# A_wq's first half in two requests (32 and 96 partitions), and the store's wait on GpSimd

## The chip, the cores and the metric

The kernel runs on one core of a Trainium2 chip, and the metric is the device time of one execution in microseconds (us), median of several runs. A core has TensorE (PE), VectorE (DVE), ScalarE (ACT), GpSimd (POOL) and SyncE (SP). Each has its own list of instructions and waits on semaphores. Transfers between device memory and the on-chip memory of 128 partitions are requested by an instruction on an engine, here nearly all on SyncE, and carried out by 16 DMA engines which all the queues share.

## The reference

One token is decoded. Its normalised row goes through a sliding-window attention (window 4096 of a cache of 65,536, 32 query heads, 8 K/V heads of 128) and through a gated feed-forward block of 1792, and both are added to the input.

```python
x = A_x                                   # (1, 1, 512)
xn = _layernorm(x, axis=-1)
return x + _A_ref(xn, A_k_cache, A_v_cache, A_wq, A_wo) + _B_ref(xn, B_w_r, B_w_gate, B_w_up, B_w_down)

# _A_ref: W = 4096, Hq = 32, Hkv = 8, Dh = 128
q = (x @ wq) split into heads             # wq: (512, 4096)
k, v = last W rows of each cache, each head repeated for 4 query heads
p = softmax(q k^T * Dh**-0.5);  o = p v
return o @ wo                             # wo: (4096, 512)

# _B_ref (S = 1, C = 1: the one token is always selected)
y = (silu(x @ w_gate) * (x @ w_up)) @ w_down
return x + y * sigmoid(x @ w_r)
```

## The kernel before

All weights and the window of the caches are read once, 30.67 MB in all, and there is little arithmetic on each byte. The kernel therefore requests everything early, on SyncE's queue, in the order in which it is needed: the two halves of `A_wq` (`wq0`, `wq1`, 2 MiB each), K in five pieces (`k0` and `k1` of 1 MiB for one head each, then three of 2 MiB for two heads each), V in four of 2 MiB, `w_gate` and `w_up` (1.75 MiB each), `A_wo` in two of 2 MiB, and `w_down` in four pieces of 896, 512, 256 and 128 KiB. The tensor `wq_sb` holds `A_wq` as 128 partitions x 4 blocks of 4096: a partition's row of one half (two blocks) is 16 KB in one piece. Two small rows, the token `x` and the router's weights `wr`, are requested on ScalarE.

The head. The program begins with a barrier of all engines. Two requests are taken out of the body and put ahead of it: `early` (line 103) records an instruction's name in `ahead`, and when the program is complete `hoist` (line 82) moves each such instruction into the first block, in front of its engine's drain, which is the engine's part in that barrier. These are `wq0` on SyncE and `x` on ScalarE (lines 110 and 111). `hoist` also moves the instructions that would end each engine's program, among them a further barrier, up to a place in the middle (`ends_at`; for SyncE behind the request `v0`).

The body. VectorE and ScalarE normalise `x` (lines 236 to 247), TensorE turns the row into a column (L251), VectorE and ScalarE compute the router's factor (L257 to L264), and TensorE spreads it (L266). Then TensorE computes q (L295), first with `wq0` (`kh` = 0), then, behind two filling products (L290), with `wq1`; before each half it waits for its transfer, by `PE.need(t_wq[kh], t_ps0)` (line 291). SyncE requests `w_gate` and `w_up` when q is complete.

The scores. For each of eight K/V heads VectorE copies K to a work buffer (`kin`, L334; it waits for the K transfer here), TensorE transposes it (L367), VectorE and ScalarE bring it back (`kT`, L339 and L342), and TensorE multiplies it with q (L376). A maximum over the window, an exponential (L425), the transposes of p (L431) and eight rounds with V (L442 to L489) follow.

The end. TensorE computes gate and up (L511), o through `A_wo` (L536), and the products with `w_down` (L541), each piece behind its own wait; fillers (L191, L489) are products whose results are not used. VectorE and ScalarE each bring half of the result row back (L568, L569), SyncE requests its store and waits for the landing (lines 571 and 572). `Eng.need` (line 27) puts a wait on that engine's own list; nothing follows this wait in any engine's program but its end.

```python
t_wq = [early(nc.sync, "wq0", wq_sb[:, 0:KH, :], wq_v[:, 0:KH, :])]
t_x = early(nc.scalar, "x", xrow[:], A_x.rearrange("a b d -> (a b) d"))
```

Of the kernel before, what the change touches and what calls it, by code (L numbers as in the profile page):

```python
# [38 lines left out]
def kernel(  # L39
# [14 lines left out]
    nc = tc.nc  # L54
    P = 128
# [18 lines left out]
    wq_sb = nc.alloc_sbuf_tensor("wq_sb", [P, KT, NQ], BF16)  # L74
    xrow = nc.alloc_sbuf_tensor("xrow", [1, D], BF16)
    KH = KT // 2
    wq_v = A_wq.rearrange("(p kt) n -> p kt n", kt=KT)

    ahead, ends_at = {}, {}

    @ctx.callback
    def hoist():
        tc.close()
        tc.compile()
        blocks = nc.main_func.blocks
        head = blocks[0].instructions
        for blk in blocks[1:]:
            for i in [i for i, o in enumerate(blk.instructions) if o.name in ahead][::-1]:
                ins = blk.instructions.pop(i)
                at = next(k for k, o in enumerate(head) if o.engine == ins.engine and isinstance(o, mybir.InstDrain))  # L90
                head.insert(at, ins)
        for eng, name in ends_at.items():
            tail = []
            for blk in blocks[-2:]:
                for o in [o for o in blk.instructions if o.engine == eng and not isinstance(o, mybir.InstUnconditionalBranch)]:
                    blk.instructions.remove(o)
                    tail.append(o)
            blk, at = next((b, k) for b in blocks for k, o in enumerate(b.instructions) if o.name == name)
            blk.instructions[at + 1:at + 1] = tail
# [3 lines left out]
    def early(eng, name, out_, in_):  # L103
        s = nc.alloc_semaphore("d_" + name)
        ins = eng.dma_start(out=out_, in_=in_)
        ins.then_inc(s, 16)
        ahead[ins.ins.name] = ins.ins.engine
        return (s, 16)

    t_wq = [early(nc.sync, "wq0", wq_sb[:, 0:KH, :], wq_v[:, 0:KH, :])]  # L110
    t_x = early(nc.scalar, "x", xrow[:], A_x.rearrange("a b d -> (a b) d"))
    W3, F1, F2, F3, F4 = 2, 2, 1, 1, 2

# [71 lines left out]
    PE, ACT, DVE, POOL, SP = (Eng(nc, nc.tensor, "pe"), Eng(nc, nc.scalar, "act"), Eng(nc, nc.vector, "dve"),  # L185
                              Eng(nc, nc.gpsimd, "pool"), Eng(nc, nc.sync, "sp"))
    te, ac, ve, gp, sy = nc.tensor, nc.scalar, nc.vector, nc.gpsimd, nc.sync
# [5 lines left out]
    def ends(ins):  # L193
        ends_at[ins.ins.engine] = ins.ins.name
        return ins

    def dma(eng, name, out_, in_):
        s = S("d_" + name)
        ins = eng.dma_start(out=out_, in_=in_)  # L199
        ins.then_inc(s, 16)  # L200
        if name == "v0":
            ends(ins)
        return (s, 16)

    t_wr = dma(ac, "wr", wr_row[:], B_w_r.rearrange("(a d) -> a d", a=1))
    t_wq.append(dma(sy, "wq1", wq_sb[:, KH:, :], wq_v[:, KH:, :]))
    TP = W // PH

    def pair(name, tile_, cache, i0, i1):
# [22 lines left out]
    t_ps0 = DVE.mark(ve.memset(ps[:, 0:2, :].rearrange("p a b -> p (a b)"), 0.0))  # L232
# [4 lines left out]
    a = DVE.mark(ve.bn_stats(out=stats[:], in_=xrow[:]))  # L237
# [6 lines left out]
    a = DVE.mark(ve.reciprocal(out=sml[:, 1:2], in_=sml[:, 0:1]))  # L244
# [5 lines left out]
    for kt in range(KT):  # L250
        ins = te.matmul(ps[:, 6, 256 + kt:257 + kt], lhsT=xn_row[:].rearrange("a (p k) -> a k p", k=KT)[:, kt, :],  # L251
                        rhs=ident_bf[0:1, 0:1], start=True, stop=True)
# [34 lines left out]
    for kh in range(2):  # L287
        if kh == 1:
            for ch in range(2):
                te.matmul(sc[:, ch, :], lhsT=zst[:], rhs=zmov[:], start=True, stop=False, skip_group_check=True)  # L290
        PE.need(t_wq[kh], t_ps0)
        for hf in range(2):
            for kt in range(kh * KH, (kh + 1) * KH):
                for c in range(4):
                    ins = te.matmul(ps[32 * c:32 * c + 1, hf, :], lhsT=xnT[:, kt:kt + 1],  # L295
                                    rhs=wq_sb[:, kt, (4 * hf + c) * 512:(4 * hf + c + 1) * 512],
                                    start=(kt == 0), stop=(kt == KT - 1), tile_position=(0, 32 * c))
            if kh == 1:
                t_qp = PE.mark(ins)
                ACT.need(t_qp)  # L300
                t_qe.append(ACT.mark(ac.copy(out=q4[:, hf, :], in_=ps[:, hf, :])))
    for hf in range(2):
# [3 lines left out]
        for hl in range(4):  # L306
            ins = te.transpose(qT_ps[:, hl, :], q4[:, hf, hl * DH:(hl + 1) * DH], ident_bf[:])
# [97 lines left out]
    a = POOL.mark(gp.memset(rf, 0.0))  # L405
# [8 lines left out]
    a = DVE.mark(ve.reduce_max(out=gm[:], in_=ps[0:2, 6, 0:P].rearrange("a (q c) -> a c q", q=8), axis=AX.X))  # L414
# [13 lines left out]
    for h in range(2):  # L428
        PE.need(t_p[h])
        for k in range(8):  # L430
            ins = te.transpose(tp[:, h, k * P:(k + 1) * P], p_sb[:, h, k * P:(k + 1) * P], ident_bf[:])  # L431
# [39 lines left out]
    with te.Fori(1, 9) as i:  # L471
# [4 lines left out]
        for tl in range(4):  # L476
            ins = te.matmul(pv_ps[32 * tl:32 * tl + 32, :], lhsT=pTcur[:, tl].rearrange("p q e r -> p (q e r)"),  # L477
                            rhs=vin[:, 0].rearrange("p (q t) d -> p t q d", t=4)[:, tl],
                            start=True, stop=False, tile_position=(0, 32 * tl))
        ins.then_inc(pe_pva, 1)  # L480
        te.wait_ge(s_vb, i)
        for tl in range(4):
            ins = te.matmul(pv_ps[32 * tl:32 * tl + 32, :], lhsT=pTcur[:, 4 + tl].rearrange("p q e r -> p (q e r)"),  # L483
                            rhs=vin[:, 1].rearrange("p (q t) d -> p t q d", t=4)[:, tl],
                            start=False, stop=True, tile_position=(0, 32 * tl))
        ins.then_inc(pe_pv, 1)
        collect(psf[:, bass.ds(4 * 512 + g * 8, 8)]).then_inc(pe_col, 1)
        for _ in range(W3):
# [9 lines left out]
    a = DVE.mark(ve.reduce_sum(out=oT_f[:].rearrange("p (g j) -> p g j", g=HP),  # L498
                               in_=ps[:, 4, 8:72].rearrange("p (g u j) -> p g j u", g=HP, u=2), axis=AX.X))
# [7 lines left out]
    for m in range(2):  # L507
        PE.need(t_g if m == 0 else t_u)
        for kt in range(KT):
            for c in range(4):  # L510
                ins = te.matmul(ps[32 * c:32 * c + 1, 2 + m, 0:FC], lhsT=xnT[:, kt:kt + 1],  # L511
                                rhs=wgu[:, m * KT * F + kt * F + c * FC:m * KT * F + kt * F + (c + 1) * FC],
                                start=(kt == 0), stop=(kt == KT - 1), tile_position=(0, 32 * c))
# [6 lines left out]
    a = ACT.mark(ac.activation(out=gth4[:], in_=ps[:, 2, 0:FC], func=ACTF.Tanh, scale=0.5))  # L520
# [13 lines left out]
    def grouped(j, lhsT, w):  # L534
        c = j % 4
        return te.matmul(a_ps[32 * c:32 * c + 1, :], lhsT=lhsT, rhs=w[:, j * D:(j + 1) * D], start=False, stop=False,  # L536
                         tile_position=(0, 32 * c), skip_group_check=True)

    def by_halves(lhsT, row, stop=False):
        for c in range(2):  # L540
            ins = te.matmul(g_ps[c], lhsT=lhsT, rhs=row[:, c * HD:(c + 1) * HD], start=False, stop=stop,  # L541
                            tile_position=(0, 32 * c), skip_group_check=True)
        return ins

    for k, (j0, j1) in enumerate(wo_chunks):
        PE.need(t_wo[k])
        for j in range(j0, j1):
            ins = grouped(j, oT2[:, j:j + 1], wo_sb)
# [8 lines left out]
    for k, (j0, j1) in enumerate(wd_chunks):  # L557
        PE.need(t_wd[k])
        for j in range(j0, j1):
            ins = by_halves(hTr[:, j, 0:1], wd_sb[:, j * D:(j + 1) * D], stop=(j == FB - 1))  # L560
# [8 lines left out]
    ac.copy(out=res[:, HD:], in_=g_ps[1]).then_inc(s_res, 1)  # L569
    sy.wait_ge(s_res, 2)  # L570
    t_out = dma(sy, "out", out.rearrange("a b d -> (a b) d"), res)
    SP.need(t_out)


# [28 lines left out]
```

## Time and profile before

| | |
|---|---|
| median of 3 runs | 79.16 us (78.93 to 79.17) |
| the profiled execution's own time | 79.16 us |
| its span, first to last instruction | 77.7 us |
| mean granted TensorE clock | 0.978 |
| read from device memory | 30.67 MB, 395 GB/s over the span |
| busy: PE, DVE, ACT, POOL | 72%, 57%, 39%, 13% |
| chain of waits: PE, DMA, ACT, DVE | 42%, 27%, 14%, 9% |

The profile is one execution, with times from the first instruction on. A row like the one of DMA cuts the span into 40 slices of 1.94 us, each digit a busy share in tenths. The timeline gives the start, the duration, the engine, the line and the operands of instructions, and in brackets how long the engine had been idle before and what ended that. "SPq" and "ACTq" are the request instructions themselves on SyncE and ScalarE, not the transfers. In the list of waits a row gives who waited for whom, the total, the number of times, and the longest. The windows give, for a stretch of the span, its length, each engine's busy time with its instructions, and at the end the granted clock, the busy share of the 16 DMA engines and the GB/s that they moved.

### The profile page before, as it was taken

To read this page: it belongs to the slowest core of one execution; us is meant where nothing else is said; L and a number is where in the kernel's file an instruction comes from. 1 tells how busy PE (TensorE), PEld (TensorE's weight loads), DVE (VectorE), ACT (ScalarE), POOL (GpSimd) and SP (SyncE) were. 2 spreads that over 40 slices of the span, in tenths; PEclk is the share of its full clock that TensorE was granted. 3 is DMA by queue.
4 is the path that set the end of the run, shared out by engine and by line. 5 is a ranking of instruction groups with operands and counts; after the bars stand their busy time and mean duration, and the time that the engine had idled before them with its cause. 6 is when DMAs were issued, how large, how long until landed. Compare 5 with 4: busy or idle time off the path is not lost.

```text
span 77.7 us, 1640 instructions
## 1 busy us (share of the span) xinstructions
PE 56.4 (72%) x642; PEld 29.7 (38%) x642; DVE 43.9 (57%) x96; ACT 30.4 (39%) x41; POOL 10.3 (13%) x22
## 2 busy tenths in 40 slices
PE   0010795489823999899799586778888779999991
PEld 0010401266603666577568122422322234343350
DVE  2763910488007876696696376398898914920302
ACT  2760002227940559589577505233334332000001
POOL 3950000003100302022021860000000000000000
PEclk9999999999999569999999999999999999999999
DMA  6899999999999999999999999999999999999910
GB/s 135 362 439 422 421 405 421 438 455 430 430 413 455 413 430 430 430 430 430 430 417 430 421 430 430 428 404 443 428 428 434 429 430 438 421 391 397 346 37 1
DMA packets 2745, 30.72 MB, mean 395 GB/s; under 512 B 307, under 2 KB 438, under 8 KB 822
## 3 DMA queue, kind: packets, MB, share of 16 engines
q1 hardware_dynamic: 2738, 30.67, 94.1%
q8 instruction: 2, 0.03, 0.2%
q14 instruction: 1, 0.01, 0.0%
q10 hardware_dynamic: 4, 0.00, 0.0%
HBM read 30.67 MB, written 0.00 MB: 395 GB/s over the span
## 4 chain that ended last, share of the span: by engine, by line
PE 42%; DMA 27%; ACT 14%; DVE 9%; issue 3%; SPq 2%; DVEq 0%
DMA k_sb<-in_A_k_cache_dram 27%; PE ps L367 13%; ACT kT L342 8%; PE ps L191 7%; PE ps L376 5%; ACT pvS L462 5%; PE ps L541 3%; PE ps L483 3%; PE ps L477 3%; PE ps L536 2%; DVE vin L448 2%; ACT kin L425 2%; PE ps L511 2%; SPq L199 2%; PE ps L468 2%
## 5 line engine op out<-in xcount | busy, mean ns | idle before, releaser
L342 ACT COPY kT<-ps 128x1024 bf16<-128x1024 bf16 x19 | 18.6, 1016 | 11.3 <-PE ps L367 11.0
L367 PE MATMUL ps<-perm_bf,kin 128*128 128x128 bf16 x256 | 18.1, 227 | 4.0 <-DVE kin L334 3.6
L367 PEld LDWEIGHTS ps<-perm_bf,kin 128*128 128x128 bf16 x256 | 15.2, 101 | 8.4 <-issue 4.4
L334 DVE COPY kin<-k_sb 128x2048 bf16<-128x2048 bf16 x16 | 10.9, 687 | 6.5 <-DMA k_sb<-in_A_k_cache_dram 4.5
L339 DVE COPY kT<-ps 128x1024 bf16<-128x1024 bf16 x13 | 9.0, 690 | 2.8 <-PE ps L367 2.3
L462 ACT CAST pvS<-ps 128x512 bf16<-128x512 f32 x8 | 4.7, 586 | 10.0 <-PE ps L468 10.0
L376 PE MATMUL ps<-kT,qAB 128*32 128x512 bf16 x68 | 7.2, 414 | 1.9 <-ACT kT L342 1.9
L327 POOL COPY qAB<-qpad 128x64 bf16<-128x64 bf16 x8 | 3.8, 477 | 33.6 <-PE ps L376 33.6
L191 PE MATMUL ps<-zmov,zst 128*128 128x512 bf16 x32 | 7.9, 381 | 0.0
L442 DVE COPY vin<-v_sb 128x2048 bf16<-128x2048 bf16 x8 | 5.5, 685 | 1.1 <-PE ps L477 0.9
L448 DVE COPY vin<-v_sb 128x2048 bf16<-128x2048 bf16 x8 | 5.5, 684 | 0.0
L477 PE MATMUL ps<-vin,pTcur 128*32 128x512 bf16 x32 | 3.2, 386 | 2.6 <-ACT pvS L462 2.2
L489 PE MATMUL ps<-zmov,zst 128*128 128x512 bf16 x16 | 4.7, 376 | 0.0
L569 ACT CAST kT<-ps 1x256 bf16<-1x256 f32 x1 | 0.4, 363 | 10.3 <-PE ps L541 10.3
L191 PEld LDWEIGHTS ps<-zmov,zst 128*128 128x128 bf16 x32 | 2.7, 98 | 3.7 <-issue 1.3
L251 PE MATMUL ps<-ident_bf,xn_row 1*128 1x1 bf16 x4 | 0.3, 165 | 5.2 <-DVE xn_row L246 5.2
L295 PE MATMUL ps<-wq_sb,xnT 128*1 128x512 bf16 x32 | 2.9, 499 | 0.8 <-DMA wq_sb<-in_A_wq_dram 0.8
L376 PEld LDWEIGHTS ps<-kT,qAB 128*32 128x32 bf16 x68 | 1.9, 93 | 4.1 <-issue 1.8
L483 PE MATMUL ps<-vin,pTcur 128*32 128x512 bf16 x32 | 3.2, 387 | 0.3 <-DVE vin L448 0.2
L477 PEld LDWEIGHTS ps<-vin,pTcur 128*32 128x32 bf16 x32 | 1.1, 92 | 6.0 <-DVE vin L442 5.5
L555 DVE TENSOR_TENSOR kT<-ps,kT 128x512 f32<-128x512 f32 x1 | 0.7, 692 | 4.4 <-PE ps L536 4.4
L447 DVE COPY pTcur<-ps 128x256 bf16<-128x256 bf16 x8 | 2.3, 285 | 1.6 <-PE ps L431 1.6
(96 smaller groups left out, 52.0 us busy)
## 6 DMA issues: line engine op xcount, KB each, us to landing
v_sb<-in_A_v_cache_dram SPq DMA_DIRECT2D x4, 2048.0 KB, 38.4
k_sb<-in_A_k_cache_dram SPq DMA_DIRECT2D x3, 2048.0 KB, 24.9
wq_sb<-in_A_wq_dram SPq DMA_DIRECT2D x2, 2048.0 KB, 9.3
k_sb<-in_A_wo_dram SPq DMA_DIRECT2D x2, 2048.0 KB, 33.6
k_sb<-in_A_k_cache_dram SPq DMA_DIRECT2D x2, 1024.0 KB, 14.1
wq_sb<-in_B_w_gate_dram SPq DMA_DIRECT2D x1, 1792.0 KB, 43.8
wq_sb<-in_B_w_up_dram SPq DMA_DIRECT2D x1, 1792.0 KB, 47.7
k_sb<-in_B_w_down_dram SPq DMA_DIRECT2D x1, 896.0 KB, 37.6
```

The source lines that it names most:

```text
L191: te.matmul(ps[:, 7, :], lhsT=zst[:], rhs=zmov[:], start=True, stop=True)
L334: ve.tensor_copy(out=kin[:, 2 * h:2 * h + 2, :], in_=k_sb[:, g, 2 * h:2 * h + 2, :]).then_inc(s_c[h], 1)
L339: ve.tensor_copy(out=kT[:, b, :], in_=tp[:, b, :]).then_inc(s_ev[b], 1)
L342: ac.copy(out=kT[:, b, :], in_=tp[:, b, :]).then_inc(s_ev[b], 1)
L367: ins = te.transpose(tp[:, b, k * P:(k + 1) * P], kin[:, b, k * P:(k + 1) * P], perm_bf[:])
L376: ins = te.matmul(sc[32 * cq:32 * cq + 32, e, :], lhsT=qAB[:, e, :], rhs=kT[:, b, :].rearrange("d (k h q) -> d h k q", h=2, q=PH)[:, e], s ...
L442: ve.tensor_copy(out=vin[:, 0].rearrange("p (q k) d -> p q (k d)", q=4), in_=v_in[:, :, 0:4 * DH]).then_inc(s_va, 1)
L448: ve.tensor_copy(out=vin[:, 1].rearrange("p (q k) d -> p q (k d)", q=4), in_=v_in[:, :, 4 * DH:]).then_inc(s_vb, 1)
L462: ac.copy(out=pvS[:].rearrange("p t d -> p (t d)"), in_=pv_ps).then_inc(s_pvs, 1)
L477: ins = te.matmul(pv_ps[32 * tl:32 * tl + 32, :], lhsT=pTcur[:, tl].rearrange("p q e r -> p (q e r)"), rhs=vin[:, 0].rearrange("p (q t) d ...
L483: ins = te.matmul(pv_ps[32 * tl:32 * tl + 32, :], lhsT=pTcur[:, 4 + tl].rearrange("p q e r -> p (q e r)"), rhs=vin[:, 1].rearrange("p (q t ...
L489: te.matmul(ps[:, 7, :], lhsT=zst[:], rhs=zmov[:], start=True, stop=True)
```

## The change

There are two edits. The first half of `A_wq` is requested by two instructions in place of one, for partitions 0 to 31 and for partitions 32 to 127, each with a semaphore of its own; both are moved ahead of the head barrier, and `hoist` keeps their order (it now inserts in front of an instruction already moved there, or of the drain; it goes through the block from its end). TensorE waits for both before the first half of q. And the wait for the landing of the result's store is on GpSimd's list in place of SyncE's; the store itself is still requested by SyncE.

```diff
-                at = next(k for k, o in enumerate(head) if o.engine == ins.engine and isinstance(o, mybir.InstDrain))
+                at = next(k for k, o in enumerate(head) if o.engine == ins.engine and (isinstance(o, mybir.InstDrain) or o.name in ahead))
                 head.insert(at, ins)
...
-    t_wq = [early(nc.sync, "wq0", wq_sb[:, 0:KH, :], wq_v[:, 0:KH, :])]
+    t_wq0 = [early(nc.sync, f"wq0{a}", wq_sb[a:b, 0:KH, :], wq_v[a:b, 0:KH, :]) for a, b in ((0, 32), (32, P))]
...
-    t_wq.append(dma(sy, "wq1", wq_sb[:, KH:, :], wq_v[:, KH:, :]))
+    t_wq = [t_wq0, [dma(sy, "wq1", wq_sb[:, KH:, :], wq_v[:, KH:, :])]]
...
-        PE.need(t_wq[kh], t_ps0)
+        PE.need(*t_wq[kh], t_ps0)
...
-    SP.need(t_out)
+    POOL.need(t_out)
```

## The prediction

> **What bounds the kernel now.** I read the page first, then the chain of waits, the waits by engine, the timeline of the first 24 and the last 15 us, and windows over the end. The page:
>
> ```profile
> DMA  6899999999999999999999999999999999999910
> q1 hardware_dynamic: 2738, 30.67, 94.1%
> DMA k_sb<-in_A_k_cache_dram 27%; PE ps L367 13%; ACT kT L342 8%; PE ps L191 7%; PE ps L376 5%; ACT pvS L462 5%; PE ps L541 3%; PE ps L483 3%; PE ps L477 3%; PE ps L536 2%; DVE vin L448 2%; ACT kin L425 2%; PE ps L511 2%; SPq L199 2%; PE ps L468 2%
> ```
>
> The DMA row is full from the third slice to the 38th: one stream of 30.67 MB, nearly all on one queue (q1, SyncE's), without a hole. The chain has one long DMA piece, 27% of the span. The timeline says which:
>
> ```profile
> 0.00 0.41 SPq L105 DMA_DIRECT2D wq_sb<-in_A_wq_dram  x1
> 1.26 0.33 SPq L199 DMA_DIRECT2D wq_sb<-in_A_wq_dram  x1
> 1.63 3.25 SPq L199 DMA_DIRECT2D k_sb<-in_A_k_cache_dram  x5
> ...
> 23.77 0.69 DVE L334 COPY kin<-k_sb 128x2048 bf16<-128x2048 bf16 x1 [4.54 <-DMA k_sb<-in_A_k_cache_dram]
> ```
>
> VectorE stands idle for 4.54 us until the third K transfer (heads 2 and 3) is there. From 24.5 us on the chain is compute, and at the end it meets the stream again:
>
> ```profile
> PEld ps L541 <- DMA k_sb<-in_B_w_down_dram: 0.4, 2, 0.2
> SPq L101 <- DMA out_dram<-kT: 0.8, 1, 0.8
> ```
>
> ```profile
> 75.00:75.50 0.50, 0.50 (x12) 0.28 (x10) 0.00 (x0) 0.00 (x0) 0.00 (x0) 1.00 0.04 14
> ```
>
> TensorE's last products wait for the last pieces of w_down, 0.2 us twice; SyncE waits 0.8 us for the store. The window's last two numbers (DMA share, GB/s) say that a single one of the 16 DMA engines is still moving bytes at 75 us: the trace's landings of the last piece come by 74.38 us from fifteen engines and at 75.77 from one. That one was also last at 23.74 us, where the other fifteen had landed the K transfer by 22.20; a 16 KB packet of another queue (q8, kind "instruction") stood before it at 21.6 us for 1.05 us. So the time hangs on the stream at both places, and on its slowest engine: what moves the stream by d moves the first compute that matters (23.77) and the last landing (75.77) by d, hence the whole time.
>
> **The change, part by part.** The profiled execution took 79.16 us, which is also the median; 77.7 are span, 1.46 lie around it. Sums are made against 79.16.
>
> (a) One more request on SyncE ahead of the head barrier. Two requests of A_wq cost 0.41 and 0.33 us of issue there; the second one here costs the same, with a gap of 0.05, so 0.37 to 0.46. In the trace SyncE's barrier arrival is at 0.58 us and ScalarE's, which has the x load before it, at 0.81; SyncE's becomes 0.95 to 1.04, so the barrier passes 0.14 to 0.23 later. All engines start that much later, wq1, the K and V requests too, and with them the second barrier of SyncE's queue, after the first V request (4.93 plus 0.63), for which VectorE's router product at 7.03 waits. Cover: wq1's request moves from 1.26 to about 1.5, while the DMA engines are busy with the first half until 6.5 to 7.1. VectorE's delay passes on to L266 and to the first q products at 8.69, which take 1.9 us and are followed by two filling products (1.0 us) up to 11.5; then TensorE waits for wq1, whose landings end at 12.32. So 0.8 us hide it: 0. Without that cover it would cost its 0.14 to 0.23. The second wait that TensorE gets before L295 is over together with the first: 0.
>
> (b) The start of the stream. The 16 engines' first packets start from 1.04 to 1.45 us, one after another; each then needs 1.05 to 1.51 us, the next ones 0.61. A first request with a quarter of the rows may be spread over the engines in a quarter of those 0.41 us: the mean engine then starts 0.15 earlier, the last 0.31, the first not at all. Its two rows an engine last past 2.8 us, and the second request, 0.37 to 0.46 later, is there by 1.9: no gap. The slow engine is the ninth or tenth to start (1.20 us). Bounds -0.3 to 0; I take -0.1.
>
> (c) The rate of transfers that touch 32 and 96 partitions. This the trace doesn't show: every large transfer in it has 128 partitions, eight 16 KB packets on each of 16 engines at 0.611 us, 26.8 GB/s each and 430 together; the only others (x, the router's row, the result) have one partition and move 1 KB in one packet of 44 to 48 ns, 22 GB/s. Bounds: if the number of partitions doesn't matter, 2.1 MB take 4.9 us as now: 0. If the rate goes with the partitions (8 rows on 4, then 12 engines), 0.52 MB at 108 and 1.57 MB at 323 GB/s take 4.9 us each: +4.9. Between them I go by doublings: from 1 to 128 partitions the rate rises from 22 to 430 in seven, 1.53 each. 32 lie two below 128: 430/1.53^2 = 184 GB/s, 2.85 us. 96 lie 0.415 of one below: 360 GB/s, 4.37 us. Sum 7.2 against 4.9: **+2.3**. Nothing takes this back later, since the engines are full to the end.
>
> [...] By the steady 0.611 us per packet alone the sum would be near 79.2. [...]
>
> (d) The wait for the store's landing goes from SyncE to GpSimd. The span still ends there: the last instruction now is SyncE's branch 0.02 us after the landing at 77.70. GpSimd's queue has only its exit behind the wait, and nothing before it since L407 ended at 45.97, so it is parked early. Its reactions in the trace take longer (L405 starts 0.19 us after the semaphore that it waited for was raised at 44.59, while SyncE's store starts 0.02 after its own). After the span a counter is raised at 76.28, 76.62, 76.65, 76.70, and for the fifth time at 77.97, after SyncE's end, then in steps of 0.04: engines report in turn, and if GpSimd stands ahead of others in that turn they follow it by 0.04 each. Bounds: -0.1 (SyncE's own 0.25 us of leaving was the longer) to +0.3; I take +0.1.
>
> Sum: 79.16 + 0 - 0.1 + 2.3 + 0.1 = 81.46, say **81.5**. Its own range takes (c) from +1.1 (about half) to +4.1 (0.8 short of the upper bound): 80.2 to 83.3.
>
> **The rivals.** *No change*: packets of 0.611 us whatever the partitions, as all steady ones here are; then 79.16 - 0.1 + 0.1 = 79.2, within 79.0 to 79.4. For it: later requests queue without a hole (wq1 behind wq0). Against: those are all alike. *Faster* (the other side): the stagger of the first packets is what matters, the slow engine starts up to 0.3 earlier, and leaving costs nothing or gains 0.1: 79.16 - 0.3 - 0.1 = 78.8. It decides if the slow engine's packets stay at 0.61 and its first one starts before 1.0; against it, x's single packet, requested later and with one row, starts at 1.00, so little lies before that. *Strict share*: rows stay eight to an engine, +4.9: 84.1. For it: eight rows an engine everywhere; against: it would leave engines empty by design. *It does less than it says*: the order of instructions shows both requests before SyncE's barrier, so this is excluded.
>
> **How the numbers follow.** What a measurement can tell from no change is about 0.3%, 0.24 us. Chances: forecast 0.62, strict share 0.08, no change 0.18, faster 0.12. Of the no-change case, 79.0 to 79.4, some 0.03 falls below by more than 0.24 us and 0.02 above: slower 0.72, same 0.13, faster 0.15. The range holds 8 in 10 from 78.9 to 83.3: it takes the forecast's own 80.2 to 83.3 and the no-change case, leaving out the strict share and most of the fast one.
>
> **What would show it.** (c): packets of 16 KB well above 0.611 us between 2.5 and 10 us; wq1's landing that TensorE waits for at L295 moved from 12.3 to about 14.5; VectorE's L334 start moved from 23.77 to about 26; a DMA row not full in slices 2 to 5. If these stay, (c) is 0 and the forecast is wrong. (b): first packets within 0.1 us of each other. (a): GpSimd's L219 at 1.4 in place of 1.24, and no more. (d): the time around the span, 1.46, grows by 0.1; SyncE's wait for the store is gone and one on GpSimd stands in its place. It would also be wrong if the instruction packet of 1.05 us met another DMA engine or another moment: that slow engine decides both waits, and its 1.4 us could vanish with any shift.

## The result, and the profile after

The changed kernel takes 83.58 us (median of 5 runs, 83.48 to 83.72) against 79.16 (5 runs, 78.91 to 79.23); the ratio is 1.0568, 95% interval 1.0544 to 1.0592. It is slower, as forecast, but by 4.42 us where 2.3 were forecast, and 0.3 us above the range.

The profiled execution of the changed kernel also took 83.58 us; of these its span is 81.6 (before: 77.7) and 1.98 lie around it (before: 1.46). So 3.9 us came into the span and 0.5 lie outside it. Its page, in the rows of the stream and of the chain:

```profile
DMA  5999999999999999999999999999999999989910
GB/s 129 257 241 241 201 345 409 413 422 430 470 417 409 458 418 409 458 418 409 458 397 409 466 401 418 466 388 446 436 414 416 469 401 418 466 374 404 392 58 1
...
DMA k_sb<-in_B_w_down_dram 47%; DMA wq_sb<-in_A_wq_dram 18%; PE ps L367 12%; ACT kT L342 4%; PE ps L376 4%; PE ps L541 3%; PE ps L295 2%; DVE kin L334 1%; PE ps L307 1%; SPq L199 1%; DVE kT L339 1%; DVE qpad L312 1%; DVE kT L568 1%; SPq L84 0%; SPq L101 0%
```

The kernel before had this GB/s row:

```profile
GB/s 135 362 439 422 421 405 421 438 455 430 430 413 455 413 430 430 430 430 430 430 417 430 421 430 430 428 404 443 428 428 434 429 430 438 421 391 397 346 37 1
```

The busy row shows nothing: the engines count as busy from the second slice on. The GB/s row shows it: 201 to 257 in slices 2 to 5 (2 to 10 us), where the kernel before moved 362 to 439, and the old rate from slice 7 on. The engines count as busy at either rate: the busy row stands at 9 at 241 GB/s as at 430. The trace's packets say the same: before, a 16 KB packet took 0.611 us from the second or third of each engine on; now those of `A_wq`'s first half, on all 16 engines alike, take about 1.1 us (0.97 to 1.29 between 3 and 10 us), and from the second or third packet of the whole-width `wq1` on they take 0.61 again. The first half's last words were written between 6.53 and 7.12 us before, and between 9.82 and 10.75 now; the last piece of `w_down` at 75.33 before on its slowest engine, now at 79.21.

The timeline answers to the rows shown of before, and to two more of the kernel before, the first of the timeline, the second of the list of waits:

```profile
1.24 0.20 POOL L219 MEMSET ident_bf<- 128x128 bf16 x1 [0.81 <-SPq L101]
PE ps L295 <- DMA wq_sb<-in_A_wq_dram: 0.8, 1, 0.8
```

Now:

```profile
0.00 0.85 SPq L105 DMA_DIRECT2D wq_sb<-in_A_wq_dram  x2
1.47 0.20 POOL L219 MEMSET ident_bf<- 128x128 bf16 x1 [1.04 <-SPq L101]
...
9.83 0.68 DVE L257 SCALAR_TENSOR_TENSOR rprod<-xn_row,wr_row 1x512 f32<-1x512 bf16 x1 [4.06 <-DMA wr_row<-in_B_w_r_dram]
...
11.90 1.88 PE L295 MATMUL ps<-wq_sb,xnT 128*1 128x512 bf16 x16 [0.34 <-DMA wq_sb<-in_A_wq_dram]
...
16.44 1.88 PE L295 MATMUL ps<-wq_sb,xnT 128*1 128x512 bf16 x16 [1.70 <-DMA wq_sb<-in_A_wq_dram]
```

TensorE's wait for `wq1` ends at 16.4 in place of 12.4 us. q is 4.1 us late, and the first two heads, for which VectorE had long been done at 23.77 before, are now still in work when the third K transfer lands (26.27 us); line L334 waits for TensorE alone. At the end TensorE again waits for the last pieces of `w_down`. The router's row, on ScalarE's queue (q10), is late too: its one packet started at 7.8 us in place of 4.9, and VectorE waits 4.06 us for it, beside the transfer that TensorE needs in any case.

### The profile page after: what moved, and what is told of

Read it like the earlier page. It is cut to its first block, busy times and chain, and to the rows that moved or that the text cites. A ratio compares the mean times of both kernels' runs of the same rounds, so it can differ in the third digit from the quotient of the medians.

```text
span 81.6 us, 1642 instructions
## 1 busy us (share of the span) xinstructions
PE 59.2 (73%) x642; PEld 31.3 (38%) x642; DVE 44.1 (54%) x96; ACT 30.6 (37%) x41; POOL 10.2 (12%) x22
## 4 chain that ended last, share of the span: by engine, by line
DMA 65%; PE 23%; ACT 4%; DVE 3%; issue 1%; SPq 1%
DMA k_sb<-in_B_w_down_dram 47%; DMA wq_sb<-in_A_wq_dram 18%; PE ps L367 12%; ACT kT L342 4%; PE ps L376 4%; PE ps L541 3%; PE ps L295 2%; DVE kin L334 1%; PE ps L307 1%; SPq L199 1%; DVE kT L339 1%; DVE qpad L312 1%; DVE kT L568 1%; SPq L84 0%; SPq L101 0%
## 5 line engine op out<-in xcount | busy, mean ns | idle before, releaser
L367 PE MATMUL ps<-perm_bf,kin 128*128 128x128 bf16 x256 | 19.4, 237 | 1.4 <-DVE kin L334 0.9
L367 PEld LDWEIGHTS ps<-perm_bf,kin 128*128 128x128 bf16 x256 | 16.5, 106 | 6.0 <-issue 4.8
L334 DVE COPY kin<-k_sb 128x2048 bf16<-128x2048 bf16 x16 | 10.9, 687 | 3.4 <-PE ps L367 3.4
L295 PE MATMUL ps<-wq_sb,xnT 128*1 128x512 bf16 x32 | 3.8, 621 | 2.0 <-DMA wq_sb<-in_A_wq_dram 2.0
L266 PE MATMUL ps<-sml,ones_f 1*128 1x1 f32 x2 | 0.6, 359 | 5.4 <-DVE sml L264 5.4
L312 DVE COPY qpad<-ps 128x16 bf16<-128x16 bf16 x4 | 0.5, 169 | 6.9 <-PE ps L307 6.9
L301 ACT CAST q<-ps 128x512 bf16<-128x512 f32 x2 | 1.2, 585 | 7.0 <-PE ps L295 7.0
```

What stands on the lines that cost most here:

```text
L334: ve.tensor_copy(out=kin[:, 2 * h:2 * h + 2, :], in_=k_sb[:, g, 2 * h:2 * h + 2, :]).then_inc(s_c[h], 1)
L367: ins = te.transpose(tp[:, b, k * P:(k + 1) * P], kin[:, b, k * P:(k + 1) * P], perm_bf[:])
```

## Experiments

The theories after the result. A: a request of fewer than 128 partitions runs slowly as such. B: the prediction's doublings. C: two requests at the head, or a second one ahead of the barrier, do it. D: the order in which rows are read does it. For the half microsecond outside the span: GpSimd's wait. Times of before are medians of runs of the kernel before on the same chip.

### The two edits apart

```diff
-    SP.need(t_out)
+    POOL.need(t_out)
```

> The kernel before with one edit: the wait for the store's landing on GpSimd in place of SyncE. Theory 1 (GpSimd leaves the program later, and engines that report behind it follow): the changed kernel's time around its span was 1.98 us against 1.46, so +0.5 us here, 79.65, with the span unchanged at 77.7. Rival (the 0.5 us belong to something else in the changed kernel, the wait's place costs the +0.1 of the prediction): 79.25.

Measured 79.61 against 79.02, ratio 1.0073 (1.0054 to 1.0093), with a span of 77.5. It is theory 1: +0.59 us, none of it in the span. The trace's counters give the course: the store landed at 77.40, GpSimd's report follows at 78.08, 0.68 us later, and the last counter of the execution 1.45 us after that. With the wait on SyncE (next run) the report follows the landing by 0.26 us, and the last counter 1.32 us after that: 0.42 us of the cost lie before the report and 0.13 behind it.

The other edit alone:

```diff
-    t_wq = [early(nc.sync, "wq0", wq_sb[:, 0:KH, :], wq_v[:, 0:KH, :])]
+    t_wq0 = [early(nc.sync, f"wq0{a}", wq_sb[a:b, 0:KH, :], wq_v[a:b, 0:KH, :]) for a, b in ((0, 32), (32, P))]
```

> The changed kernel with the store's wait back on SyncE: the split into 32 and 96 partitions alone. If the two edits add up: 83.58 - 0.5 = 83.1, ratio to before 1.050, the 16 KB packets of both requests at 1.1 us as in the changed kernel. If the GpSimd wait costs only 0.1, 83.5.

Measured 83.08 against 79.02, ratio 1.0514 (1.0456 to 1.0572): +4.06. The two add up: 0.59 + 4.06 = 4.65 against the 4.42 of both, within the width of the intervals (the second reaches from +3.6 to +4.5).

### Is it two requests, or their partitions?

Two requests of the same sizes, cut along the rows:

```diff
+    t_wq0 = [early(nc.sync, "wq0a", wq_sb[:, 0, 0:NQ // 2], wq_v[:, 0, 0:NQ // 2]),
+             early(nc.sync, "wq0b", bass.AP(wq_sb, NQ // 2, [[KT * NQ, P], [1, 3 * NQ // 2]]),
+                   A_wq.rearrange("(p kt) n -> p (kt n)", kt=KT)[:, NQ // 2:2 * NQ])]
```

> The same bytes in two requests of the same sizes (0.52 and 1.57 MB), both ahead of the barrier, but cut along the rows: 128 partitions each, 4 KB and 12 KB of each row; store's wait on SyncE. Theory A (the number of partitions of a request sets its rate): full rate, time as before within 0.3 us, 78.9 to 79.4, start of VectorE's L334 wait end near 23.7. Rival C (two requests in flight at the head, or a second one ahead of the barrier, halve the rate whatever their shape): 83.1 as with the split by partitions.

Measured 78.94 against 79.02, ratio 1.0009 (0.9977 to 1.0041). C falls: a second request ahead of the barrier costs nothing that can be measured. It brings nothing either: the first half's last words came between 6.54 and 6.96 us.

The split at partition 64 (`((0, 64), (64, P))` in the edit of the second run):

> The split at partition 64 (0 to 63, 64 to 127), both ahead of the barrier, store's wait on SyncE. Theory A in the form 'any request with fewer than 128 partitions runs at a bit over half the rate, however many it has': packets of 1.1 us and the same +3.9, 83.1. Rival B, the prediction's doublings (281 GB/s for 64 partitions, 7.5 us in place of 4.9): +2.6, 81.8. Full rate, if 32 was the trouble: 79.2.

Measured 84.26 against 79.02, ratio 1.066 (1.064 to 1.0679): +5.24, worse than 32 and 96, with packets of 1.15 to 1.30 us between 3 and 10 us. Its windows over the first half, the last number the GB/s:

```profile
2.00:4.00 2.00, 0.00 (x0) 0.00 (x0) 1.64 (x4) 1.49 (x2) 1.69 (x6) 1.00 1.18 270
4.00:6.00 2.00, 0.08 (x3) 0.11 (x4) 1.34 (x4) 1.71 (x3) 1.87 (x2) 1.00 0.76 156
6.00:8.00 2.00, 0.18 (x4) 0.10 (x3) 0.16 (x1) 0.07 (x1) 0.00 (x0) 1.00 1.14 246
8.00:10.00 2.00, 0.00 (x0) 0.00 (x0) 0.00 (x0) 0.00 (x0) 0.00 (x0) 1.00 0.92 189
```

215 GB/s on the mean, half of the stream. B falls: it had 64 partitions faster than 32, and 81.8. A in this form isn't met either, with 83.1.

### Ten requests by themselves

> A kernel that computes nothing: it loads ten pieces of A_wq, 16 KB a row, one after the other, each waited for before the next, and stores one row of the last as a result. In order: all 128 partitions; 0 to 31; 32 to 127; 32 to 63; 0 to 63; 64 to 127; 0 to 15; every eighth partition (16 of them); every second (64); all 128 again. Packet times beyond each request's first. [...] Theory A2 (any request of fewer than 128 partitions is slow in the same way, 1.1 to 1.2 a packet, wherever it lies): 0 to 15 and every eighth take the same time. Rival D (it is the order in which the rows are read from device memory): no difference between the partitions that a request writes, only between the rows that it reads.

The list of requests, with their size and the time from issue to landing:

```profile
all_rows<-in_A_wq_dram SPq DMA_DIRECT2D x1, 2048.0 KB, 7.3
all_again<-in_A_wq_dram SPq DMA_DIRECT2D x1, 2048.0 KB, 7.2
upper_three<-in_A_wq_dram SPq DMA_DIRECT2D x1, 1536.0 KB, 8.7
lower_half<-in_A_wq_dram SPq DMA_DIRECT2D x1, 1024.0 KB, 7.6
upper_half<-in_A_wq_dram SPq DMA_DIRECT2D x1, 1024.0 KB, 7.5
every_second<-in_A_wq_dram SPq DMA_DIRECT2D x1, 1024.0 KB, 5.0
first_quarter<-in_A_wq_dram SPq DMA_DIRECT2D x1, 512.0 KB, 4.7
second_quarter<-in_A_wq_dram SPq DMA_DIRECT2D x1, 512.0 KB, 4.7
first_sixteen<-in_A_wq_dram SPq DMA_DIRECT2D x1, 256.0 KB, 4.0
every_eighth<-in_A_wq_dram SPq DMA_DIRECT2D x1, 256.0 KB, 3.5
```

Half of the partitions take longer than all of them, if they are neighbours (7.6 and 7.5 against 7.3 us); partitions 32 to 127, three quarters of the bytes, take 8.7. The same megabyte to every second partition takes 5.0. Packets after each engine's first: median 0.611 us for all 128 and for every second; 1.28 for 0 to 63, 1.27 for 64 to 127, 1.14 and 1.20 for the two quarters, 1.09 for 32 to 127. So A2 falls, the number of partitions isn't it: every second, 64 partitions, has the full rate, and 0 to 15 is 0.39 us longer in its packets than every eighth (means of 1.30 and 0.91), where A2 had the two alike.

### What is written, or what is read

> The kernel before, its first request of 128 partitions reading the rows of A_wq in another order (partition 4a+c gets row 32c+a, so that engines at work together read neighbouring rows, as with 32 partitions); q is computed from permuted weights. Theory A (what is written matters): packets 0.61 us, VectorE's L334 at 23.8, 79.1 us. Rival D (what is read matters): packets towards 1.1 us in the first half, up to +4, 83.

```diff
-    t_wq = [early(nc.sync, "wq0", wq_sb[:, 0:KH, :], wq_v[:, 0:KH, :])]
+    t_wq = [early(nc.sync, "wq0", wq_sb[:, 0:KH, :], A_wq.rearrange("(c a kt) n -> a c kt n", c=4, kt=KT)[:, :, 0:KH, :])]
```

The packets kept their 0.61 us (0.61 to 0.79 after each engine's first two), and the first half's last words came between 6.75 and 7.40. VectorE's wait for K ended at 22.5, earlier than expected, since the instruction packet that held up one engine at 21.6 us in the kernel before came at 45.1 here. So D falls, if engines at work together then read neighbouring rows; that was the author's estimate, and no run shows which rows an engine takes. The time, 80.14 in one run against 79.01, isn't explained by this: its windows show a granted clock of 0.50 between 68 and 70 us, where the run before had 1.00, and TensorE waited 2.2 us for `A_wo`. What lowered the clock wasn't looked into.

> The kernel before with the third K transfer (heads 2 and 3, 2 MiB, in the middle of the stream, 16 KB a row, its source one piece of memory without gaps) requested for partitions 0 to 31 and 32 to 127; A_wq as before. Theory A: this transfer's packets take 1.1 us, it lands 3.5 to 4 later, VectorE's L334 wait ends near 27.5 and the time is 82.6 to 83. If only the head of the stream, or A_wq's source with its gaps, is slow that way: 0.61 and 79.2.

```diff
+        if name == "k" and i0 == 2:
+            row = HKV * NT * DH
+            toks = [dma(sy, f"{name}{i0}_{a}", bass.AP(tile_, i0 * NT * DH + a * row, [[row, z - a], [1, n * DH]]),
+                        src[a // 2:z // 2, :, t0:t0 + n, :].rearrange("q h t d -> q h (t d)")) for a, z in ((0, 32), (32, P))]
+            return [toks] * (i1 - i0)
...
-            DVE.need(t_k[g])
+            DVE.need(*(t_k[g] if isinstance(t_k[g], list) else [t_k[g]]))
```

Measured 83.98 in one run, against 79.01. The timeline at the wait for that transfer (the copy L334 is line 339 here), and two windows of the stream:

```profile
28.15 0.69 DVE L339 COPY kin<-k_sb 128x2048 bf16<-128x2048 bf16 x1 [7.51 <-DMA k_sb<-in_A_k_cache_dram]
```

```profile
18.00:20.00 2.00, 2.00 (x24) 1.71 (x20) 1.37 (x3) 0.76 (x2) 0.35 (x1) 0.59 1.00 229
20.00:22.00 2.00, 2.00 (x33) 1.50 (x30) 0.64 (x1) 2.00 (x3) 0.24 (x1) 1.00 0.88 197
```

The wait ends at 28.15 in place of 23.77 and the stream falls to 200 to 230 GB/s, now in its middle and from a source without gaps. Theory A, as stated for this run, holds in another place; the last engine had again an instruction packet (1.36 us, at 25.6) before its last ones.

### Where the partitions lie

> Nothing computed again; eight requests one after the other: every second partition from 64 neighbouring rows; partitions 0 to 63 from every second row; partitions 32 to 95; partitions 0, 2 to 62 (32 of them); partitions 0 to 15 with 32 KB each, from memory without gaps; every eighth partition with 32 KB each; partitions 0 to 3 with 32 KB each; all 128. The first series: 0 to 63 and 64 to 127 1.28 us a packet, every second one 0.611. Theory H (each half of the memory, partitions 0 to 63 and 64 to 127, takes some 215 GB/s, half of the stream, however many partitions a request writes in it): 0.61, 1.25, 0.61, 1.2, 1.2, 0.61, and for four partitions, with at most 4 engines, 0.61 a packet. [...] Theory S (the rows read matter): first request 1.25, second 0.61.

```profile
spread_from_near<-in_A_wq_dram SPq DMA_DIRECT2D x1, 1024.0 KB, 5.5
lower_from_spread<-in_A_wq_dram SPq DMA_DIRECT2D x1, 1024.0 KB, 7.7
middle<-in_A_wq_dram SPq DMA_DIRECT2D x1, 1024.0 KB, 5.2
lower_every_second<-in_A_wq_dram SPq DMA_DIRECT2D x1, 512.0 KB, 5.0
sixteen_near<-in_A_k_cache_dram SPq DMA_DIRECT2D x1, 512.0 KB, 6.4
sixteen_apart<-in_A_k_cache_dram SPq DMA_DIRECT2D x1, 512.0 KB, 4.6
```

The first two rows settle D: rows lying near, written to every second partition, 5.5 us; rows lying apart, written to 0 to 63, 7.7. Partitions 32 to 95 are neighbours too, and take 5.2: half of them lie below 64 and half above. Partitions 0, 2 to 62 lie below 64 and are slow (median 1.21 us a packet), those of the middle take 0.611. That is theory H, for requests of 32 partitions and more that lie within one half or in equal parts in both: what they write within 0 to 63, or within 64 to 127, gets about half of the stream (1.14 to 1.28 us a packet beside 0.611). It doesn't say why 32 to 127, which lie in both, had 1.09 us a packet. For fewer partitions it isn't enough: sixteen neighbours took 3.6 us for a 32 KB packet, where H allowed twice 1.2 and the start, sixteen apart 2.0, and four neighbours 3.25, where H allowed 1.2 beside the start. What binds there beside the halves stays open.

The test in the kernel, 64 and 64 partitions again, but the even and the odd ones:

```diff
+    t_wq0 = [early(nc.sync, f"wq0{a}", wq_sb[a:P:2, 0:KH, :], wq_v[a:P:2, 0:KH, :]) for a in range(2)]
```

> The kernel before with A_wq's first half in two requests ahead of the barrier, even and odd partitions, 64 each, all other things as before. Theory H: each request spreads its engines over both halves of the memory, so packets stay at 0.611 us and the time at 78.8 to 79.3 (0 to 63 and 64 to 127 cost 84.26). If fewer than 128 partitions are slow in any case: 83 to 84.3.

Measured 79.13 against 79.11, ratio 0.9991 (0.9957 to 1.0025). Its page:

```profile
GB/s 127 397 406 415 406 418 427 431 473 414 414 431 473 431 414 406 422 448 448 418 422 406 422 439 456 406 399 444 436 392 493 404 431 406 422 412 402 393 35 1
```

The stream is whole again from the second slice, with packets of 0.61. The same two requests of 64 partitions cost 5.2 us or nothing, by where the partitions lie.

### The half microsecond at the end

```diff
-    SP.need(t_out)
+    DVE.need(t_out)
```

> The kernel before with the wait for the store's landing on VectorE, which reports at the end behind GpSimd and ahead of SyncE. Where the +0.6 of GpSimd's wait comes from: if from its place in the order of reports (the rest follows in steps of 0.04), +0.05, 79.1; if any engine but SyncE leaves its program slowly after a wait, +0.5, 79.6; if GpSimd alone is slow to leave (0.68 us from the landing to its report in the changed kernel, 0.27 on SyncE), 79.0 to 79.2.

Measured 79.10 against 79.11, ratio 0.9986 (0.9953 to 1.002). VectorE reports 0.35 us after the landing. So not every engine other than SyncE leaves slowly: GpSimd does (0.68 us from the landing to its report, beside 0.26 on SyncE). TensorE and ScalarE weren't tried.

## Why the prediction was wrong

**What bounds the kernel** was right for the end: the stream. What moved it by 3.9 us (the last word of `w_down`'s last piece from 75.33 to 79.21) moved the span by 3.9. The other place, VectorE's wait for K, did not set the time. The run with GpSimd's wait alone was profiled in an execution in which no instruction packet came before 30 us; there the wait was short, and the chain goes through `w_down` and `wq1` (a row of the list of waits, then the page's chain):

```profile
DVE kin L334 <- DMA k_sb<-in_A_k_cache_dram: 0.9, 1, 0.9
DMA k_sb<-in_B_w_down_dram 51%; DMA wq_sb<-in_A_wq_dram 14%; PE ps L367 10%; ACT kT L342 6%; PE ps L541 3%; PE ps L376 3%; PE ps L295 2%; DVE kin L334 2%; PE ps L307 1%; SPq L199 1%; DVE kT L339 1%; DVE qpad L312 1%; DVE kT L568 1%; SPq L84 0%; SPq L101 0%
```

K came 1.7 us earlier than in the profiled execution of the kernel before (22.0 in place of 23.7 us), and the span was 77.5 beside 77.7. So two of the signs that the prediction named could not come: L334's wait for K doesn't move with the stream, it vanishes, and the DMA row stays full at half the rate.

**(c), the rate of the partial transfers**, is the step that failed, by its size: 4.37 us for 96 partitions and 2.85 for 32, together +2.3, where the split alone cost 4.06. The doublings took the number of partitions for the cause, so that 96 came out nearly as fast as 128, at 360 GB/s; and they began at a packet of 1 KB on one engine (22 GB/s), so that the size of the packet went into the step as well. In the changed kernel, by the means over the 16 engines, the six packets of the second request took 6.77 us together in place of 3.71, +3.1, where the prediction had +0.7; the two of the first took 2.25 in place of 1.95, +0.3, where it had +1.6; and the first packet of `wq1` behind them took 1.03 in place of 0.61, +0.4. That makes 3.8 of the 3.9 us by which `wq1`'s last words are late (15.43 to 15.90 us in place of 11.40 to 11.99). So the term for 96 partitions was much too small and the one for 32 too large, and the sum is nearer than its parts by luck. By themselves the 96 had 217 GB/s over the request, beside 350 for all 128. From the first packet's start to the last word 0 to 31 had 184 GB/s by themselves and 0 to 63 192 (0.5 and 1 MiB), and 0 to 15 had 126 (32 KB to each). Why the 96 are as slow as that stays open (see the last section). The split alone, at 83.08, would have lain inside the range, near its end; (d) carried the time out of it.

**(d), the wait on GpSimd**, was taken as +0.1 within -0.1 to +0.3, and costs 0.59. The order of reports was read rightly; the engine's own way out was priced by a row of another kind, the 0.19 us that GpSimd took from a semaphore to its next instruction. From the landing to its report it takes 0.68, SyncE 0.26; the rest of the cost lies in the counters behind the report.

**(b), the earlier start,** gave nothing: the 16 engines' first packets started from 1.02 to 1.93 us, not closer together than the 1.04 to 1.45 of before. **(a)** was right in its sum: the barrier passes 0.23 later (L219 at 1.47 in place of 1.24) and nothing on the path feels it; the split along the rows, which has the same extra request, measures 1.0009. That TensorE's two waits before the first half of q end together was not: the first request had landed by 4.83 us, the second by 11.76, and q began at 11.90 in place of 8.69. The wait for `wq1` behind it, 1.70 us, hides that.

**The rivals.** No change and faster fell with the first profile. Strict share, at 84.1, is the nearest of the four cases, but for a wrong reason: no engine stood empty, all 16 were slow together.

## What to carry to other kernels

Cut a transfer along the row (78.94 us against 79.02), or into partitions that lie in both halves (even and odd, or 32 to 95), and not into a block within partitions 0 to 63 or 64 to 127: two requests of 64 partitions cost 5.2 us in the one case (0 to 63 and 64 to 127) and nothing in the other (even and odd). That a request reaches into both halves isn't enough: 32 to 127 was slow (1.09 us a packet). 32 to 95 was tried only by itself (0.611). Look at GB/s and at the duration of packets, since the DMA engines counted as busy at half their rate (9 in the busy row at 241 GB/s as at 430). Let SyncE or VectorE wait for the last store (79.11 and 79.10 us); on GpSimd the same wait cost 0.6 us.

## What the runs showed beside it

The request for partitions 32 to 127 is slow on all 16 engines alike, 1.1 us a packet, although two thirds of its rows lie in the upper half and a third in the lower; alone it took 8.7 us, longer than all 128 partitions. If each engine wrote in one half and were bound only by it, a third of them should have been faster. When the request ran alone, the engines' second packets still took 0.63 us in the median, and the slow ones began with the third (means of 1.02 to 1.18). Which rows each engine takes, and what ties the engines together, wasn't tried; so the cause of most of the 3.9 us is known as far as the request that lost them, and not beyond.

The slowest DMA engine is the one with an instruction packet in its way: in the run before 1.05 us at 21.6 us, and the next transfers landed 1.4 to 1.5 us later on one engine than on the other fifteen; in the changed kernel 1.06 at 40.8, with the split K transfer 1.36 at 25.6. It came at another moment in each of these runs, and where it falls before a wait decides which transfer is seen as late.
